# A GQA and gMLP block on one core: the second unit's queries a slot earlier, the second chunk's norm in two parts, and the last output tile in halves

## The chip, the cores and the metric

The kernel runs on one core of a Trainium2 chip. The metric is the device time of one launch in microseconds (us), the median of several runs. TensorE (PE) does the matmuls, ScalarE (ACT) the exponentials, VectorE (DVE) most copies out of PSUM and the norms, GpSimd (POOL) some small steps, and SyncE (SP) issues nearly all DMAs. Each engine works through its own instructions in program order.

## The reference, cut to what matters

```python
mod = (silu(c) @ w_mod)                        # sa, ca, ga, sb, cb, gb: 512 values each
h = layernorm(x) * (1 + ca) + sa               # x: 2048 x 512
x = x + ga * A(h)                              # attention: 32 query heads, 8 key/value heads of 128,
                                               # 2048 cached keys; wq 512 x 4096, wo 4096 x 512
h = layernorm(x) * (1 + cb) + sb
x = x + gb * B(h)                              # gMLP:
    z  = gelu(h @ w_in)                        #   512 x 1792
    z1, z2 = z[:, :896], layernorm(z[:, 896:])
    B  = (z1 * (w_sp @ z2 + b_sp)) @ w_out     #   w_sp 2048 x 2048, w_out 896 x 512
```

## The kernel before, in words

**Units and slots.** The 2048 rows are cut into 16 tiles of 128, four tiles make a chunk of 512 (`CT = 4`). Attention is 128 units: key/value group g (of 8) by tile j, with the group's four query heads together. The main loop runs over iterations `it` (0 to 133), each of eight slots. In a slot stand, in this order: what was put down for it with `at(it, slot, fn)` (kept in `later`), the score matmuls and the exponential of unit `it` (`qk`, s_ps banks, two of them), a part of the probabilities-times-values matmuls of an earlier unit (`pv`, `pv_rows`, o_ps banks), the `fill` of the slot (the query projections, `qproj`, misc banks), and the output projection of an earlier unit (`wo_proj`, misc banks). The schedule is manual: each engine runs its instructions in exactly this order, and an engine that waits holds back all that is behind it on its queue.

**Two kinds of units.** Units 5 to 121 go by rows in two cases of three: ACT writes the probabilities by rows, and SP turns them with four DMA transposes per unit (`turn_rows`, line 1088). The other units work by columns and need no such turn, but their outputs are turned (line 1147).

**The start.** Chunk 0 is normalised in pieces so that unit 0 can begin early. Queries of tiles 2 and 3 (`rest_q`) are projected as 16 matmuls of 256 columns in the fills of iteration 1, and DVE copies them to `qT` (line 978) in two parts. Chunks 1 to 3 go through `ln1_at`: statistics, `ln1_norm` (four normalised tiles `xn1`), a slot later `ln1_dma` (four DMA transposes from SP into `hT`, line 836), later `ln1_dma_mod` (DVE scales and shifts the whole chunk in place, four instructions, line 805 through `ln1_mod`). For chunk 1 these stand in (0, 7), (1, 2), (1, 3) and (2, 2). The query projection of chunk 1 starts in the fill of (2, 5) and ends in (3, 4). A load of 2 MB of modulation weights (`wmod_b`, which lies in the tile `wsp`; line 1312) stands at (1, 4) on the same SP queue.

**The second norm.** In the last group, `ln2` normalises each finished tile: `first` takes the statistics, `second` (slot 4 of the next iteration) normalises to `xn2` on DVE and turns it by DMA from SP to `xnT2` (line 1219), `third` (an iteration later, slot 3) modulates it on DVE (line 1226).

**The end.** The last 512 rows of the gMLP are worked off in a part of 384 columns and a part of 128 (`spatial`, 16 matmuls and one for the bias each). For the last 128, seven steps f make `yT[:, f]` on DVE (line 1573), and `o2_mm` sums seven matmuls of 512 columns into one bank; `finish_tile` multiplies by `gb_rows` (line 1590), adds x (line 1591) and issues the output's DMA from ACT's queue.

Of the kernel before, what the change touches and what calls it, by code (L numbers as in the profile page):

```python
# [10 lines left out]
BF16 = mybir.dt.bfloat16  # L11
FP32 = mybir.dt.float32
ACT = mybir.ActivationFunctionType
ALU = mybir.AluOpType
AX = mybir.AxisListType
P = 128
# [559 lines left out]
def kernel(  # L576
# [19 lines left out]
    nc = tc.nc  # L596
    _, S, D = A_x.shape
# [7 lines left out]
    NT = S // P  # L605
    NDT = D // P
    NKT = SK // P
    NFT = FH // P
    NCH = S // 512
    CT = 512 // P  # L610
# [8 lines left out]
    out_dram = out[0].rearrange("(t p) d -> p t d", p=P)  # L619
# [26 lines left out]
    x_sb = res.tile([P, NT, D], BF16, name="x_sb")  # L646
    ga_rows = res.tile([P, D], FP32, name="ga_rows")
    gb_rows = res.tile([P, D], FP32, name="gb_rows")
# [20 lines left out]
    def bank(name):  # L669
        return psum.tile([P, 512], FP32, name=name)  # L670
# [4 lines left out]
    def rstd_of(mv, n, tag):  # L675

        ve = stat.tile([P, CT], FP32, name=f"ve_{tag}")
        nc.gpsimd.tensor_scalar(
            out=ve[:, :n], in0=mv[:, :, 1], scalar1=LN_EPS, scalar2=None, op0=ALU.add
        )  # L680
        rstd = stat.tile([P, CT], FP32, name=f"rstd_{tag}")
        nc.gpsimd.tensor_tensor(out=rstd[:, :n], in0=ve[:, :n], in1=mhalf[:, :n], op=ALU.pow)
        return rstd

    def normalise(dst, src, mv, rstd):
        nc.vector.tensor_scalar(
            out=dst,
            in0=src,
            scalar1=mv,
            scalar2=rstd,  # L690
            op0=ALU.subtract,
            op1=ALU.mult,
        )

    def ln_stats(mv, j, src):
        st = stat.tile([P, 1, nc.vector.BN_STATS_DIM], FP32, name="bnst")
        nc.vector.bn_stats(out=st[:, 0, :], in_=src)
        nc.vector.bn_aggr(out=mv[:, j, :], in_=st[:])
# [87 lines left out]
    def ln1_stats(j0, n):  # L786
        for j in range(j0, j0 + n):
            ln_stats(mv1, j, x_sb[:, j, :])
        return rstd_of(mv1[:, j0 : j0 + n, :], n, "ln1")

    def ln1_norm(j0, n, rstd):
        xns = []
        for j in range(j0, j0 + n):
            xn = res.tile([P, D], BF16, name="xn1", bufs=4)
            normalise(xn[:], x_sb[:, j, :], mv1[:, j, 0:1], rstd[:, j - j0 : j - j0 + 1])
            xns.append(xn)
        return xns

    def hT_of(ch):
        if ch not in hTs:  # L800
            hTs[ch] = res.tile([P, NDT, 512], BF16, name="hT", bufs=NCH)
        return hTs[ch]

    def ln1_mod(dst, src, dt, engine=nc.vector):
        engine.tensor_scalar(
            out=dst,
            in0=src,
            scalar1=modc[:, NDT + dt : NDT + dt + 1],
            scalar2=modc[:, dt : dt + 1],
            op0=ALU.mult,  # L810
            op1=ALU.add,
        )
# [20 lines left out]
    def ln1_dma(j0, n, xns):  # L833
        hT = hT_of(j0 // CT)
        for jj in range(n):
            nc.sync.dma_start_transpose(out=hT[:, :, jj * P : (jj + 1) * P], in_=xns[jj][:])

    def ln1_dma_mod(ch):
        for dt in range(NDT):
            ln1_mod(hTs[ch][:, dt, :], hTs[ch][:, dt, :], dt)  # L840
# [79 lines left out]
    for dt in range(NDT):  # L920
        dst, src = hTs[0][:, dt, 0:P], xT0[:, dt * P : (dt + 1) * P]
        if dt == 1:
            nc.scalar.activation(
                out=dst,
                in_=src,
# [56 lines left out]
    first = {}  # L982
# [30 lines left out]
    def at(it, slot, fn):  # L1013
        later.setdefault((it, slot), []).append(fn)
# [191 lines left out]
    def ln2(it, j):  # L1206

        st = {}

        def first():  # L1210
            if j < NT - CT:
                ln_stats(mv2, j, x_sb[:, j, :])
            st["rstd"] = rstd_of(mv2[:, j : j + 1, :], 1, "ln2")

        def second():
            xn = res.tile([P, D], BF16, name="xn2", bufs=2)
            normalise(xn[:], x_sb[:, j, :], mv2[:, j, 0:1], st["rstd"][:, 0:1])
            st["xnT"] = res.tile([P, NDT, P], BF16, name="xnT2", bufs=2)
            nc.sync.dma_start_transpose(out=st["xnT"][:], in_=xn[:])

        def third():
            ch, c0 = j // CT, (j % CT) * P
            if ch not in h2Ts:
                h2Ts[ch] = res.tile([P, NDT, 512], BF16, name="hT", bufs=NCH)
            for dt in range(NDT):
                nc.vector.tensor_scalar(
                    out=h2Ts[ch][:, dt, c0 : c0 + P],
                    in0=st["xnT"][:, dt, :],
                    scalar1=modc[:, 4 * NDT + dt : 4 * NDT + dt + 1],
                    scalar2=modc[:, 3 * NDT + dt : 3 * NDT + dt + 1],  # L1230
                    op0=ALU.mult,
                    op1=ALU.add,
                )

        at(it + 1, 0 if j >= NT - CT else 2, first)
        at(it + 1, 4, second)
        at(it + 2, 3, third)

    mod_b = {}
# [40 lines left out]
    fill = {}  # L1280
# [16 lines left out]
    fill[0, 4], fill[0, 5] = next_q[0:8], next_q[8:16]  # L1297
    rest_q = qproj(0, [0, 1], 2 * P, 2 * P) + qproj(0, [2, 3], 2 * P, 2 * P)
    for i in range(6):
        fill[1, i + 1] = rest_q[(8 * i + 2) // 3 : (8 * i + 10) // 3]  # L1300

    def ln1_at(ch, stats, norm, turn):
        st = {}
        at(*stats, lambda: st.update(r=ln1_stats(ch * CT, CT)))
        at(*norm, lambda: st.update(x=ln1_norm(ch * CT, CT, st["r"])))
        at(norm[0], norm[1] + 1, lambda: ln1_dma(ch * CT, CT, st["x"]))
        at(*turn, lambda: ln1_dma_mod(ch))

    ln1_at(1, (0, 7), (1, 2), (2, 2))
    ln1_at(2, (2, 4), (3, 1), (4, 5))  # L1310
    ln1_at(3, (3, 5), (4, 1), (5, 5))
    at(1, 4, lambda: nc.sync.dma_start(out=wmod_b, in_=wmod_dram[:, :, 2 * D : NMOD]))
# [34 lines left out]
    for g in range(1, HKV):  # L1347
        it = (g - 1) * NT
# [6 lines left out]
        last = it - 1  # L1355
        for from_it, load in loads:
# [3 lines left out]
            last = next(u for u in pauses if u >= it + from_it and u > last)  # L1360
# [94 lines left out]
    for it in range(NU + 6):  # L1455
# [34 lines left out]
        for u in wos:  # L1490
            if u >= (HKV - 1) * NT:
                ln2(it, u % NT)
        if it == NU + 2:
            free_b.close()
            mlp = fast.enter_context(tc.tile_pool(name="mlp", bufs=1, side="right"))
            zs["z1T"] = mlp.tile([P, NFT, S], BF16, name="z1T")
            wout_sb = mlp.tile([P, NFT, D], BF16, name="wout_sb")
# [14 lines left out]
    for f in range(NFT):  # L1512
# [6 lines left out]
        out=ok1[:], in0=rall[:], scalar1=1.0 / SAFE, scalar2=None, op0=ALU.is_ge  # L1519
# [8 lines left out]
        out=bad[:], in0=okm[:], scalar1=-1.0, scalar2=1.0, op0=ALU.mult, op1=ALU.add  # L1528
# [48 lines left out]
    def o2_mm(dst, yT, jj, f):  # L1577
        nc.tensor.matmul(  # L1578
            dst,
            lhsT=yT[:, f, jj * P : (jj + 1) * P],  # L1580
            rhs=wout_sb[:, f, :],
            start=(f == 0),
            stop=(f == NFT - 1),
        )

    def finish_tile(t, jj, src):
        j = t * CT + jj
        tmp = mlp.tile([P, D], FP32, name="tmp", bufs=2)[:].bitcast(BF16)[:, 0:D]
        yout = mlp.tile([P, D], BF16, name="yout", bufs=2)
        nc.vector.tensor_tensor(out=tmp[:], in0=src, in1=gb_rows[:], op=ALU.mult)  # L1590
        nc.vector.tensor_tensor(out=yout[:], in0=tmp[:], in1=x_sb[:, j, :], op=ALU.add)
        nc.scalar.dma_start(out=out_dram[:, j, :], in_=yout[:])
# [3 lines left out]
    def o2_tile(t, jj):  # L1596
        o2 = bank("o_ps")
        for f in range(NFT):
            o2_mm(o2[:], yTs[t], jj, f)
        finish_tile(t, jj, o2[:])  # L1600

    last = NCH - 1
# [16 lines left out]
    o2_last = [acc[jj // 2][:, (jj % 2) * 512 : (jj % 2 + 1) * 512] for jj in range(CT)]  # L1619
    yT = yTs[last]  # L1620
    for f in range(NFT):
        spatial(last, yT, f, 0, n_a)
        if f < CT:
            o2_tile(last - 1, f)
        if f > 0:
            for jj in range(CT - 1):
                o2_mm(o2_last[jj], yT, jj, f - 1)
    redo = nc.values_load(flag[0:1, 0:1], min_val=0, max_val=P)
    for f in range(NFT):
        spatial(last, yT, f, n_a, P, bias_by_pe=True)  # L1630
        if f == 0:
            for jj in range(CT - 1):
                o2_mm(o2_last[jj], yT, jj, NFT - 1)
        elif f < CT:
            o2_mm(o2_last[CT - 1], yT, CT - 1, f - 1)
        if f % 2 == 0 and f < 2 * (CT - 1):
            finish_tile(last, f // 2, o2_last[f // 2])
    for f in range(CT - 1, NFT):
        o2_mm(o2_last[CT - 1], yT, CT - 1, f)
    finish_tile(last, CT - 1, o2_last[CT - 1])  # L1640
    fast.close()

    with tc.If(redo != 0):
# [34 lines left out]
```

## Time and profile before

| | |
|---|---|
| median of 3 runs | 1306.26 us (1305.87 to 1306.64) |
| the profiled execution's own time | 1306.41 us |
| its span in the trace | 1304.6 us |
| PE busy | 1287.9 us, 99% |
| ACT busy | 1113.4 us, 85% |
| DVE busy | 684.1 us, 52% |
| DMA queue of SP (q1) | 87.0% of 16 engines' span |

The profile is one execution. An engine is busy while an instruction runs on it; overlapping matmuls count once. A row of the timeline gives start, length, engine, line, operation, output and inputs, shapes and count, and in brackets the idle time before it with what ended it. `SPq` rows are the issue of a DMA by SP, not its transfer; the time from issue to landing is listed with the DMA issues. A row that merges several instructions has their count at its end.

### The profile page before, as it was taken

Reading aid. Unit: us, or ns where it says so; the run is one execution under the profiler, and the core shown is the slowest. Engines: PE = TensorE matmul, PEld = TensorE weight load, DVE = VectorE, ACT = ScalarE, POOL = GpSimd, SP = SyncE. Lnnn points to the kernel's source line nnn. Section 1 sums busy time; section 2 is a strip of 40 time slices with the busy share of each in tenths; the row PEclk is TensorE's granted clock in tenths of the full one; section 3 lists DMA queues with packets and bytes.
Section 4 is the critical chain, followed back from the end, with each engine's and each line's share of the span. In section 5 each row is a group of like instructions: output and inputs, shape, how many; then the busy total and the mean of one; then the engine's idle time right before and its main releaser. Section 6 shows DMA issues by size and latency. Waiting matters only on the chain.

```text
span 1304.6 us, 22478 instructions
## 1 busy us (share of the span) xinstructions
PE 1287.9 (99%) x8472; PEld 698.1 (54%) x8626; DVE 684.1 (52%) x1772; ACT 1113.4 (85%) x1683; POOL 57.4 (4%) x93
## 2 busy tenths in 40 slices
PE   8999999999999999999999999999999999999998
PEld 6655555555555555555555555555555556644445
DVE  5635445544554455445544554455445566784443
ACT  7999999999999999999999999999999998650000
POOL 1000000000000000000000000000000133410000
PEclk9999999999999999999999999999999999999999
DMA  7899899999999999999999999999999983264300
GB/s 187 183 198 189 157 190 182 190 170 189 181 194 168 188 173 184 183 181 183 185 188 173 183 187 189 172 185 176 177 198 163 168 151 90 49 137 98 81 21 31
DMA packets 774982, 211.19 MB, mean 162 GB/s; under 512 B 759248, under 2 KB 773200, under 8 KB 774864
## 3 DMA queue, kind: packets, MB, share of 16 engines
q1 hardware_dynamic: 772416, 207.55, 87.0%
q10 hardware_dynamic: 2448, 2.10, 0.5%
q8 instruction: 70, 1.15, 0.4%
q14 instruction: 48, 0.39, 0.1%
HBM read 21.37 MB, written 2.10 MB: 18 GB/s over the span
## 4 chain that ended last, share of the span: by engine, by line
PE 95%; DVE 2%; ACT 1%; DMA 1%; issue 1%; POOL 0%; SPq 0%; ACTq 0%
PE s_ps L1031 21%; PE o_ps L1103 20%; PE o_ps L1124 14%; PE s_ps L1068 13%; PE misc L1181 8%; PE misc L967 8%; PE misc L1545 7%; PE o_ps L1578 1%; PE s_ps L1411 1%; PE s_ps L1372 1%; DVE stz L1394 1%; PE s_ps L1578 0%; DMA wmod_a<-in_w_mod_dram 0%; ACT pT L1075 0%; DMA xnT<-xn 0%
## 5 line engine op out<-in xcount | busy, mean ns | idle before, releaser
L1031 PE MATMUL s_ps<-kT,qT 128*128 128x512 bf16 x1219 | 364.9, 379 | 2.3
L1038 ACT ACTIVATE win_sb<-s_ps 128x1024 bf16<-128x1024 f32 x312 | 319.2, 1024 | 3.8 <-PE s_ps L1031 0.7
L1103 PE MATMUL o_ps<-pT,v 128*128 128x512 bf16 x909 | 272.5, 379 | 1.3
L1174 DVE SCALAR_TENSOR_TENSOR xacc<-misc,rall,xacc 128x512 f32<-128x512 f32 x304 | 227.4, 748 | 68.2 <-PE misc L1181 60.7
L1068 PE MATMUL s_ps<-qT,kT 128*128 128x512 bf16 x784 | 233.2, 379 | 1.9 <-ACT pT L1075 1.1
L1075 ACT ACTIVATE pT<-s_ps 128x1024 bf16<-128x1024 f32 x216 | 217.8, 1025 | 12.9 <-PE s_ps L1068 4.9
L1038 ACT ACTIVATE pn<-s_ps 128x1024 bf16<-128x1024 f32 x208 | 213.0, 1024 | 2.0 <-PE s_ps L1031 0.5
L1103 PEld LDWEIGHTS <-v 128*128 128x128 bf16 x1248 | 122.1, 98 | 147.3
L1075 ACT ACTIVATE wsp<-s_ps 128x1024 bf16<-128x1024 f32 x176 | 179.9, 1024 | 12.1 <-PE s_ps L1068 4.2
L1181 PE MATMUL misc<-wo_g,oT 128*128 128x512 bf16 x479 | 181.5, 379 | 1.0
L967 PE MATMUL misc<-hT,wq_g 128*128 128x512 bf16 (+2 forms) x499 | 179.6, 370 | 0.5
L1031 PEld LDWEIGHTS <-qT 128*128 128x128 bf16 x1248 | 121.5, 98 | 109.4 <-issue 0.4
L978 DVE CAST qT<-misc 128x512 bf16<-128x512 f32 x127 | 87.2, 687 | 151.2 <-PE misc L967 151.2
L1124 PEld LDWEIGHTS <-pT 128*128 128x128 bf16 x1792 | 119.6, 98 | 50.5
L1092 DVE TENSOR_TENSOR tot<-rs 128x1 f32<-128x1 f32 x312 | 48.4, 155 | 171.5 <-ACT win_sb L1038 115.2
L1124 PE MATMUL o_ps<-v,pT 128*128 128x129 bf16 x1792 | 137.5, 220 | 0.6
L1068 PEld LDWEIGHTS <-kT 128*128 128x128 bf16 x784 | 75.6, 98 | 83.0 <-DVE qT L978 1.5
L1124 PEld LDWEIGHTS <-wsp 128*128 128x128 bf16 x1408 | 94.3, 98 | 41.5
L1124 PE MATMUL o_ps<-v,wsp 128*128 128x129 bf16 x1408 | 108.5, 220 | 0.5
L1038 ACT ACTIVATE wmod_a<-s_ps 128x1024 bf16<-128x1024 f32 x104 | 106.4, 1024 | 0.4 <-PE s_ps L1031 0.4
L1545 PE MATMUL misc<-wsp,z 128*128 128x512 bf16 (+2 forms) x554 | 100.1, 336 | 0.4
L1103 PE MATMUL o_ps<-wsp,v 128*128 128x512 bf16 x292 | 87.8, 379 | 0.4
(111 smaller groups left out, 874.3 us busy)
## 6 DMA issues: line engine op xcount, KB each, us to landing
wo_g<-in_A_wo_dram SPq DMA_DIRECT2D x8, 512.0 KB, 5.0
wq_g<-in_A_wq_dram SPq DMA_DIRECT2D x7, 512.0 KB, 4.0
v<-in_A_v_cache_dram SPq DMA_DIRECT2D x7, 512.0 KB, 4.5
wsp<-in_w_mod_dram SPq DMA_DIRECT2D x1, 2048.0 KB, 8.7
out_dram<-yout ACTq DMA_DIRECT2D x16, 128.0 KB, 1.7
pT<-win_sb SPq DMA_TRANSPOSE x117, 4.8
win_sb<-in_B_w_in_dram SPq DMA_DIRECT2D x1, 1792.0 KB, 8.0
x_sb<-in_A_x_dram SPq DMA_DIRECT2D x3, 512.0 KB, 7.0
```

What stands on the lines that cost most here:

```text
L967: nc.tensor.matmul(ps[0][:, o0 : o0 + n], lhsT=wqs[g][:, dt, hh * DH : (hh + 1) * DH], rhs=hTs[ch][:, dt, c0 : c0 + n], start=(dt == 0), s ...
L978: nc.vector.tensor_copy(out=dst, in_=src)
L1031: nc.tensor.matmul(s_ps[:, c * 512 : (c + 1) * 512], lhsT=qTs[b][:, hh, jj * P : (jj + 1) * P], rhs=groups[g]["kT"][:, k0 : k0 + 512], sta ...
L1038: nc.scalar.activation(out=rows_of(u, hh)[:, half * HK : (half + 1) * HK], in_=s_ps[:], func=ACT.Exp, scale=inv_sqrt_dh, accum_out=rsums[u ...
L1068: nc.tensor.matmul(s_ps[:, h * 512 : (h + 1) * 512].rearrange("p (r q) -> p r q", r=REP), lhsT=groups[g]["kT"][:, kt * P : (kt + 1) * P], ...
L1075: nc.scalar.activation(out=pTs[u][:, 2 * i : 2 * i + 2, :], in_=s_ps[:].rearrange("p (k q) -> p k q", k=2), func=ACT.Exp, scale=inv_sqrt_dh,)
L1092: nc.vector.tensor_tensor(out=tot[:], in0=rs[:, 2 * hh : 2 * hh + 1], in1=rs[:, 2 * hh + 1 : 2 * hh + 2], op=ALU.add)
L1103: nc.tensor.matmul(o_pss[u][:], lhsT=groups[g]["v1"][:, kt, 0:DH], rhs=pTs[u][:, kt, :], start=(kt == 0), stop=(kt == NKT - 1),)
L1124: nc.tensor.matmul(o_ps[:, hh % 2, 0 : DH + 1], lhsT=pTs[u][:, kt, hh * P : (hh + 1) * P], rhs=groups[g]["v1"][:, kt, 0 : DH + 1], start=( ...
L1174: nc.vector.scalar_tensor_tensor(out=xa[:], in0=X_ps[:], scalar=scale, in1=xa[:], op0=ALU.mult, op1=ALU.add)
L1181: nc.tensor.matmul(ps[0][:], lhsT=oTs[u][:, hh, :], rhs=groups[g]["wo"][:, hh, :], start=(hh == 0 or each), stop=(hh == REP - 1 or each),)
L1545: nc.tensor.matmul(g_pss[f][:, :n], lhsT=z2[:, st, f * P : (f + 1) * P], rhs=wsp[t][:, st, c0 : c0 + n], start=(st == 0), stop=(st == NT - ...
```

## The change

- The fills of `rest_q` move from slots 1 to 6 of iteration 1 to slots 0 to 5.
- Chunk 1's norm no longer goes through `ln1_at`. Two tiles are normalised and their two DMA transposes issued at (1, 3), the other two at (1, 6). `ln1_dma` now takes a column offset. Statistics and `ln1_dma_mod` stay at (0, 7) and (2, 2). The 2 MB load stays at (1, 4), so two of the four transposes now stand behind it on SP's queue.
- `ln2`: the DMA transpose moves from `second` (slot 4) to a step of its own, `turn`, in slot 5.
- The last tile's seven matmuls of 512 columns become 14 of 256, in two banks (the second an o_ps bank); the last ones run in the order given. DVE multiplies by halves, then adds and stores the whole tile.

```diff
     def ln1_dma(j0, n, xns):
         hT = hT_of(j0 // CT)
         for jj in range(n):
-            nc.sync.dma_start_transpose(out=hT[:, :, jj * P : (jj + 1) * P], in_=xns[jj][:])
+            c0 = (j0 + jj) % CT * P
+            nc.sync.dma_start_transpose(out=hT[:, :, c0 : c0 + P], in_=xns[jj][:])
...
         def second():
             xn = res.tile([P, D], BF16, name="xn2", bufs=2)
             normalise(xn[:], x_sb[:, j, :], mv2[:, j, 0:1], st["rstd"][:, 0:1])
+            st["xn"] = xn
+
+        def turn():
             st["xnT"] = res.tile([P, NDT, P], BF16, name="xnT2", bufs=2)
-            nc.sync.dma_start_transpose(out=st["xnT"][:], in_=xn[:])
+            nc.sync.dma_start_transpose(out=st["xnT"][:], in_=st["xn"][:])
...
         at(it + 1, 4, second)
+        at(it + 1, 5, turn)
         at(it + 2, 3, third)
...
     for i in range(6):
-        fill[1, i + 1] = rest_q[(8 * i + 2) // 3 : (8 * i + 10) // 3]
+        fill[1, i] = rest_q[(8 * i + 2) // 3 : (8 * i + 10) // 3]
...
-    ln1_at(1, (0, 7), (1, 2), (2, 2))
+    at(0, 7, lambda: first.update(r=ln1_stats(CT, CT)))
+    at(1, 3, lambda: first.update(x=ln1_norm(CT, 2, first["r"])))
+    at(1, 3, lambda: ln1_dma(CT, 2, first["x"]))
+    at(1, 6, lambda: first.update(y=ln1_norm(CT + 2, 2, first["r"][:, 2:CT])))
+    at(1, 6, lambda: ln1_dma(CT + 2, 2, first["y"]))
+    at(2, 2, lambda: ln1_dma_mod(1))
...
+    halves = [slice(hf * D // 2, (hf + 1) * D // 2) for hf in range(2)]
+    o2_half_ps = [o2_last[CT - 1][:, 0 : D // 2], bank("o_ps")[:, 0 : D // 2]]
+
+    def o2_half(hf, f):
+        nc.tensor.matmul(
+            o2_half_ps[hf],
+            lhsT=yT[:, f, (CT - 1) * P : CT * P],
+            rhs=wout_sb[:, f, halves[hf]],
+            start=(f == 0),
+            stop=(f == NFT - 1),
+        )
...
         elif f < CT:
-            o2_mm(o2_last[CT - 1], yT, CT - 1, f - 1)
+            for hf in range(2):
+                o2_half(hf, f - 1)
...
-    for f in range(CT - 1, NFT):
-        o2_mm(o2_last[CT - 1], yT, CT - 1, f)
-    finish_tile(last, CT - 1, o2_last[CT - 1])
+    for hf, f in ((0, 3), (0, 4), (0, 5), (1, 3), (1, 4), (0, 6), (1, 5), (1, 6)):
+        o2_half(hf, f)
+    j_end = NT - 1
+    tmp = mlp.tile([P, D], FP32, name="tmp", bufs=2)[:].bitcast(BF16)[:, 0:D]
+    yout = mlp.tile([P, 512], BF16, name="gb", bufs=2)
+    for hf in range(2):
+        nc.vector.tensor_tensor(
+            out=tmp[:, halves[hf]], in0=o2_half_ps[hf], in1=gb_rows[:, halves[hf]], op=ALU.mult
+        )
+    nc.vector.tensor_tensor(out=yout[:], in0=tmp[:], in1=x_sb[:, j_end, :], op=ALU.add)
+    nc.scalar.dma_start(out=out_dram[:, j_end, :], in_=yout[:])
```

## The prediction

> **What bounds the kernel now.** I read the page first, then the waits, then the timeline around each edit, then the landing times of the DMAs there.
>
> ```profile
> span 1304.6 us, 22478 instructions
> PE 1287.9 (99%) x8472; PEld 698.1 (54%) x8626; DVE 684.1 (52%) x1772; ACT 1113.4 (85%) x1683; POOL 57.4 (4%) x93
> PEld L1068 <- DVE qT L978: 1.5, 1, 1.5
> DVE hT L805 <- DMA hT<-xn: 4.6, 1, 4.6
> ```
>
> TensorE is busy 1287.9 of 1304.6 us. So work taken off another engine is worth nothing, and any wait on TensorE's own queue lengthens the span in full. The last two rows are waits between 14 and 60 us: PE's weight load stands 1.5 us for a query copy just as unit 2 begins, the only moment in that stage at which PE's queues wait; and DVE stands 4.6 us for the transposes of chunk 1, which PE does not feel. The first is what the start edit can take away; the second is what it puts at risk.
>
> **The start.** The timeline of that stage:
>
> ```profile
> 23.36 1.38 DVE L686 TENSOR_SCALAR xn<-x_sb,mv,rstd_ln 128x512 bf16<-128x512 bf16 x4 [0.98 <-POOL rstd_ln L682]
> 23.80 5.90 SPq L836 DMA_TRANSPOSE hT<-xn  x4
> 25.79 0.68 DVE L978 CAST qT<-misc 128x512 bf16<-128x512 f32 x1
> 26.53 0.61 PE L1068 MATMUL s_ps<-qT,kT 128*128 128x512 bf16 x2 [1.05 <-ACT pT L1075]
> 27.23 5.60 ACT L1075 ACTIVATE pT<-s_ps 128x1024 bf16<-128x1024 f32 x6 [0.70 <-PE s_ps L1068]
> 29.75 0.59 SPq L1312 DMA_DIRECT2D wsp<-in_w_mod_dram  x1
> 30.43 8.06 SPq L1147 DMA_TRANSPOSE oT<-onorm  x2
> 31.04 1.38 DVE L805 TENSOR_SCALAR hT<-hT,modc 128x512 bf16<-128x512 bf16 x4 [4.57 <-DMA hT<-xn]
> 31.94 0.59 PE L967 MATMUL misc<-hT,wq_g 128*128 128x512 bf16 x2
> ```
>
> DVE norms four tiles before it copies queries; the second copy ends at 25.79 + 0.68 = 26.47 and PE starts unit 2 at 26.53. With the fills a slot earlier, the copy stands behind two norms instead of four and its matmuls end about a slot sooner, so unit 2 starts when ACT frees a bank: ACT's idle 0.70 us is the most that can go. I put the gain at 0.5, since the fill that now stands in slot 0 delays unit 1's second scores a little. It is worth this only if nothing stops PE later, and something does.
>
> Chunk 1's query projection starts at 31.94, behind DVE's modulation, which starts at 31.04 when the last of four transposes has landed; its first quarter takes 1.38 / 4 = 0.35. PE's slack there is thus about 0.5 us. After the change SP's order is two transposes, the 2 MB load, the other two transposes, then oT. What a transpose behind that load costs, the trace of before shows once, with the oT at 30.43:
>
> ```profile
> 23.80 3.27 SPq L836 DMA_TRANSPOSE hT<-xn  x2
> wsp<-in_w_mod_dram SPq DMA_DIRECT2D x1, 2048.0 KB, 8.7
> oT<-onorm SPq DMA_TRANSPOSE x1, 9.8
> DMA to landing us min/median/max: 2.4/2.4/4.6
> DMA packets 490, 0.13 MB, mean 125 GB/s; under 512 B 490, under 2 KB 490, under 8 KB 490
> DMA packets 100, 0.41 MB, mean 410 GB/s; under 512 B 0, under 2 KB 0, under 8 KB 100
> DMA packets 154, 0.39 MB, mean 395 GB/s; under 512 B 61, under 2 KB 61, under 8 KB 154
> ```
>
> The first row is SP's issue of two of the transposes; the next two are issue to landing of the load and of that oT; the fourth is the same for the twelve transposes of hT. The last three are what moved in 28 to 29, 35 to 36 and 36 to 37 us. A transpose is 0.13 MB in small packets, some 1 us of transfer, and lands 2.4 us after its issue. Behind the load it took 9.8: up to 36 us only large packets moved, and the oT's first small ones came when the load drained. The queue is worked off in order.
>
> So: two transposes issue by 23.80 + 3.27 = 27.07, the load at 27.1 instead of 29.75, and it lands at 27.1 + 8.7 = 35.8. The third transpose lands as the oT did, 30.43 + 9.8 - (29.75 + 8.7) = 1.8 after the load, at 37.6; the fourth one transfer later, about 0.8, at 38.4. DVE waits for it at (2, 2), and with DVE wait everything behind on its queue: unit 1's normalisation, chunk 2's statistics, the query copies. PE runs on to the fill of (2, 5) and stands there until 38.4 + 0.35 + 0.1 = 38.85, against 31.94: **+6.9 us**. The 0.5 gained ahead of it only makes PE wait longer. Nothing later gives this back: PE has no other wait up to 60 us in which to catch up, and ACT, which runs behind PE's scores, goes idle meanwhile. Bounds: the small packets came from 36 to 37 us on, up to 2 us before the load had landed; if both transposes slip into that tail, the fourth lands about 36.9 and PE loses 5.4; if the two queue behind each other with the oT's whole 1.8 each, 39.4 and 7.9. I take the value between, from the oT's own row.
>
> Then PE has stood for some 7 us, and how it restarts no row of the middle shows. The nearest is the kernel's beginning:
>
> ```profile
> 1.18 4.87 PE L777 MATMUL o_ps<-onorm 128*128 128x512 bf16 x11 [1.18 <-DVE onorm L768]
> 3.00:4.00 1.00, 1.00 (x4) 0.31 (x3) 0.89 (x4) 0.21 (x1) 0.00 (x0) 1.00 0.89 293
> 1283.47 0.81 PE L1578 MATMUL s_ps<-wout_sb,yT 128*128 128x512 bf16 x3
> ```
>
> Eleven matmuls of 512 columns took 4.87 us after idleness, 0.44 each; late in the kernel three take 0.81, of which the last one alone 0.38, so 0.215 each. The granted clock in the windows stands at 1.00 (the last but two number) even then, so the spacing shows this and not that column. PE lost 4.87 - 11 x 0.215 = 2.5 us in that start. The stage after (2, 5) is full of PE work, so the same slow stretch would cost **+2.5**; the other end is 0, if 7 us of standing does not slow it. I take 2.5, the only row there is. [...]
>
> **The second norm's turn.** On SP's queue, the slot between lets one transpose of probabilities pass ahead of xnT in three iterations; everywhere else the order is as it was. One such place is tight:
>
> ```profile
> 1061.01 1.86 SPq L1219 DMA_TRANSPOSE xnT<-xn  x1
> 1062.96 3.04 SPq L1088 DMA_TRANSPOSE pT<-wmod_a  x1
> 1065.90 0.98 DVE L1226 TENSOR_SCALAR hT<-xnT,modc 128x128 bf16<-128x128 bf16 x4 [1.44 <-DMA xnT<-xn]
> 1066.80 0.68 DVE L978 CAST qT<-misc 128x512 bf16<-128x512 f32 x1
> 1067.53 0.38 PE L1181 MATMUL misc<-wo_g,oT 128*128 128x512 bf16 x1
> 1066.00:1068.00 2.00, 2.00 (x11) 0.82 (x9) 2.00 (x7) 1.95 (x3) 0.00 (x0) 1.00 1.13 206
> ```
>
> DVE already waits 1.44 us for xnT, then copies queries until 1066.80 + 0.68 = 1067.48, and PE's matmul into a misc bank starts at 1067.53, right behind: no slack. A transpose of 0.5 MB at 206 GB/s (the last number) is 2.5 us of transfer ahead of xnT. PE then loses between 0 (the queue has a gap there that absorbs it) and 2.5; I take the middle, **+1.2**. The first of the three, and below it the second:
>
> ```profile
> 1034.10 1.60 SPq L1219 DMA_TRANSPOSE xnT<-xn  x1
> xnT<-xn SPq DMA_TRANSPOSE x1, 2.8
> 1038.25 0.97 DVE L1226 TENSOR_SCALAR hT<-xnT,modc 128x128 bf16<-128x128 bf16 x4
> 1039.14 0.68 DVE L978 CAST qT<-misc 128x512 bf16<-128x512 f32 x1
> 1041.27 0.38 PE L1181 MATMUL misc<-wo_g,oT 128*128 128x512 bf16 x1
> 1048.74 1.19 SPq L1219 DMA_TRANSPOSE xnT<-xn  x1
> 1055.69 0.97 DVE L1226 TENSOR_SCALAR hT<-xnT,modc 128x128 bf16<-128x128 bf16 x4
> ```
>
> The first landed at 1036.9, 1.3 ahead of its use; 2.5 later makes DVE 1.1 late, and the copy that frees a misc bank ends at 1040.9, still ahead of PE's next request for one at 1041.27. The second is issued 7 us ahead of its use. Both cost nothing; without that cover the first would add up to 1.1, which the upper end's full 2.5 at the tight place allows for.
>
> **The last tile.**
>
> ```profile
> 1298.75 0.29 DVE L1573 TENSOR_TENSOR yT<-misc,z1T 128x128 bf16<-128x128 f32 x1 [0.35 <-PE misc L1565]
> 1299.62 0.69 DVE L1590 TENSOR_TENSOR tmp<-s_ps,gb_rows 128x512 bf16<-128x512 f32 x1 [0.57 <-PE s_ps L1578]
> 1300.34 0.42 DVE L1591 TENSOR_TENSOR yout<-tmp,x_sb 128x512 bf16<-128x512 bf16 x1
> 25.45 0.42 DVE L1136 TENSOR_TENSOR onorm<-o_ps,rall 128x256 bf16<-128x256 f32 x1
> ```
>
> The last yT is ready at 1299.04, so the first half's last matmul can start about 1299.1 and end near 1299.4 instead of 1299.6. Two half multiplications of 0.42 follow one another, then the same addition of 0.42: the end comes at about 1300.65 instead of 1300.76, **-0.1**. The seven added matmuls split columns that were there; their weight loads run beside other matmuls. If three of them show, it is +0.2.
>
> **Sum.** 6.9 + 2.5 + 1.2 - 0.1 = 10.5, on the profiled execution's own time of 1306.41, which lies 0.15 above the median of the runs; on the median, 1306.26 + 10.5 = **1316.8 us**. A measurement here tells from no change about 0.2%, 2.6 us.
>
> **Rivals.**
>
> *PE restarts at full speed.* All else as above: 1306.26 + 6.9 + 1.2 - 0.1 = 1314.3, down to 1306.26 + 5.4 - 0.1 = 1311.6 with the lower bounds and no loss at xnT. For it: the granted clock stays at 1.00 in every window. Against: it did so in the slow start too. Chance 0.24.
>
> *The transposes are not held by the load* (not slower). If their small packets are served beside the load's large ones, each lands 2.4 after its issue. Four issues took 5.90 and two 3.27, so 1.3 each; behind the load's issue of 0.59 the fourth is issued at about 29.0 and lands at 31.4. PE then starts chunk 1's queries at 31.85, 0.1 earlier than before, xnT falls in its gap, and the time is 1306.26 - 0.1 - 0.1 = 1306.1, no measurable change. Each us that it lands later is a us lost; from a landing at 34 on it would measure as slower. Against: the 9.8 and the packet sizes. Chance 0.08.
>
> *DVE's backlog bites again.* DVE resumes with four modulations, the statistics of chunk 2 and two copies to do; if a misc bank is freed later than PE asks for it, PE stands a second time by 1 to 3 us, and 1316.8 becomes about 1319. In before, DVE and PE kept the same distance after 31.94, which speaks against. Chance 0.07.
>
> **How the numbers follow.** The forecast has 0.61. The range goes from 1311.6 to 1306.26 + 7.9 + 2.5 + 2.5 = 1319.2, which leaves out the rival without a hold and part of the backlog. Faster by over 0.2%: 0.02, since even the whole 0.70 and the last tile are under 2.6 us; within 0.2%: 0.08; slower: 0.90.
>
> **What would show it.** In the profile after: the load issued near 27.1; hT's slowest landing near 9 us instead of 4.6; a DVE wait of about 12 us at line 805's chunk modulation, up from 4.6; PE idle for about 7 us before the projection of chunk 1, with the 512-column matmuls behind it at 0.44 instead of 0.215 for some us; at about 1075 us a PE wait of 0 to 2.5 on a misc bank. If hT's landings stay under 4 us and PE has no idle stretch by 40 us, the prediction is wrong at its main term.

## The result, and the profile after

The changed kernel takes 1314.18 us (median of 6 runs, 1313.04 to 1314.94) against 1306.45 us before (6 runs, 1305.87 to 1306.96): a ratio of 1.0059, 95% interval 1.0046 to 1.0072. It is 7.7 us slower. Its profiled execution took 1314.26 us with a span of 1312.4, which is 7.8 more than before.

The page of the changed kernel, and from its waits the three that before did not have at this length (PE's own for the whole span, DVE's between 15 and 60 us; the columns are us in total, times, longest):

```profile
span 1312.4 us, 22494 instructions
PE 1290.6 (98%) x8481; PEld 700.1 (53%) x8633; DVE 685.1 (52%) x1773; ACT 1113.4 (85%) x1683; POOL 57.5 (4%) x93
PE misc L968 <- DVE hT L805: 5.1, 1, 5.1
PE misc L1182 <- DVE qT L979: 1.0, 1, 1.0
DVE hT L805 <- DMA hT<-xn: 10.2, 1, 10.2
```

PE has 2.7 us more busy time, though it multiplies no more columns, and two new waits of 5.1 and 1.0 us. The timeline of the start (lines have moved by one: 967 is now 968):

```profile
24.10 0.69 DVE L979 CAST qT<-misc 128x512 bf16<-128x512 f32 x1
25.87 0.59 PE L1069 MATMUL s_ps<-qT,kT 128*128 128x512 bf16 x2 [0.32 <-ACT pT L1076]
26.39 0.58 SPq L1322 DMA_DIRECT2D wsp<-in_w_mod_dram  x1
27.07 2.65 SPq L837 DMA_TRANSPOSE hT<-xn  x2
30.88 0.61 PE L1125 MATMUL o_ps<-v,pT 128*128 128x129 bf16 x8
36.13 1.38 DVE L805 TENSOR_SCALAR hT<-hT,modc 128x512 bf16<-128x512 bf16 x4 [10.16 <-DMA hT<-xn]
36.60 1.01 PE L968 MATMUL misc<-hT,wq_g 128*128 128x512 bf16 x2 [5.10 <-DVE hT L805]
37.40 1.06 PE L1069 MATMUL s_ps<-qT,kT 128*128 128x512 bf16 x2
39.12 1.06 PE L968 MATMUL misc<-hT,wq_g 128*128 128x512 bf16 x2
41.90 0.59 PE L1069 MATMUL s_ps<-qT,kT 128*128 128x512 bf16 x2
```

Unit 2 starts at 25.87 instead of 26.53, so the step that was meant to be quicker is. Then PE stands from 31.49 (30.88 + 0.61) to 36.60, because DVE's modulation starts at 36.13 instead of 31.04. A pair of matmuls then takes 1.01 to 1.06 us and no longer 0.59, until about 41.2. Chunk 1's query projection starts 4.7 us later than before (36.60 against 31.94); its sixth matmul is followed by scores at 41.90 against 35.01, 6.9 later. The row of before:

```profile
35.01 0.59 PE L1068 MATMUL s_ps<-qT,kT 128*128 128x512 bf16 x2
```

The step from 4.7 to 6.9, 2.2 us, is the slow stretch.

The windows of that stretch (us, then busy time and count of PE, PEld, DVE, ACT and POOL, the granted clock, the DMA share and GB/s):

```profile
33.00:34.00 1.00, 0.00 (x0) 0.00 (x0) 0.00 (x0) 0.00 (x0) 0.00 (x0) 1.00 0.99 330
34.00:35.00 1.00, 0.00 (x0) 0.00 (x0) 0.00 (x0) 0.00 (x0) 0.00 (x0) 0.69 1.47 174
40.00:41.00 1.00, 1.00 (x5) 0.44 (x4) 0.97 (x3) 0.00 (x0) 0.00 (x0) 0.50 0.00 0
41.00:42.00 1.00, 0.95 (x11) 0.77 (x10) 0.93 (x5) 0.93 (x1) 0.58 (x2) 0.89 0.00 0
```

The clock is halved: a mean of 0.69 in 34 to 35 puts the fall at about 34.4, and 0.89 in 41 to 42 puts the return at about 41.2.

The landings (load, all four transposes, and the fourth alone):

```profile
wsp<-in_w_mod_dram SPq DMA_DIRECT2D x1, 2048.0 KB, 8.6
DMA to landing us min/median/max: 2.4/5.0/8.5
hT<-xn SPq DMA_TRANSPOSE x1, 7.6
```

The load lands at 26.39 + 8.6 = 35.0, the third transpose at 27.07 + 8.5 = 35.6, the fourth, issued at 28.4, at 36.0.

The second norm's turn, at the place that had no slack:

```profile
1066.77 2.66 SPq L1089 DMA_TRANSPOSE pT<-wmod_a  x1
1069.52 1.57 SPq L1223 DMA_TRANSPOSE xnT<-xn  x1
1073.79 0.98 DVE L1230 TENSOR_SCALAR hT<-xnT,modc 128x128 bf16<-128x128 bf16 x4 [2.43 <-DMA xnT<-xn]
1074.68 0.68 DVE L979 CAST qT<-misc 128x512 bf16<-128x512 f32 x1
1075.42 0.38 PE L1182 MATMUL misc<-wo_g,oT 128*128 128x512 bf16 x1 [0.96 <-DVE qT L979]
```

The transpose of probabilities goes first, DVE waits 2.43 us instead of 1.44, and PE waits 0.96 for the bank that the query copy frees. Relative to before this matmul is 7.89 us late (1075.42 against 1067.53), up from 6.90 some us ahead of it (1067.82 against 1060.92).

The end:

```profile
1306.65 0.29 DVE L1583 TENSOR_TENSOR yT<-misc,z1T 128x128 bf16<-128x128 f32 x1 [0.35 <-PE misc L1575]
1307.32 0.42 DVE L1667 TENSOR_TENSOR tmp<-s_ps,gb_rows 128x256 bf16<-128x256 f32 x1 [0.38 <-PE s_ps L1642]
1307.66 0.42 DVE L1667 TENSOR_TENSOR tmp<-o_ps,gb_rows 128x256 bf16<-128x256 f32 x1
1308.11 0.42 DVE L1670 TENSOR_TENSOR gb<-tmp,x_sb 128x512 bf16<-128x512 bf16 x1
```

From the last yT to the end of the addition it takes 1.88 us (1306.65 to 1308.53) against 2.01 before (1298.75 to 1300.76): -0.13. So 4.7 + 2.2 + 1.0 - 0.1 = 7.8, the whole difference of the spans.

### The profile page after: what moved, and what is told of

Read it like the earlier page. It is cut to its first block, busy times and chain, and to the rows that moved or that the text cites. A ratio compares the mean times of both kernels' runs of the same rounds, so it can differ in the third digit from the quotient of the medians.

```text
span 1312.4 us, 22494 instructions
## 1 busy us (share of the span) xinstructions
PE 1290.6 (98%) x8481; PEld 700.1 (53%) x8633; DVE 685.1 (52%) x1773; ACT 1113.4 (85%) x1683; POOL 57.5 (4%) x93
## 4 chain that ended last, share of the span: by engine, by line
PE 96%; DVE 1%; DMA 1%; ACT 1%; issue 1%; POOL 0%; SPq 0%; ACTq 0%; DVEq 0%
PE s_ps L1032 20%; PE o_ps L1104 20%; PE o_ps L1125 14%; PE s_ps L1069 12%; PE misc L1182 8%; PE misc L968 8%; PE misc L1555 7%; PE s_ps L1382 2%; PE s_ps L1421 2%; PE o_ps L1588 1%; DMA hT<-xn 1%; PE o_ps L777 0%; PE s_ps L1588 0%; DMA xnT<-xn 0%; ACT pn L1039 0%
```

## The experiments

Nine kernels were run, each timed against the kernel before on the same chip.

**The load behind all four transposes.** In the changed kernel:

```diff
-    at(1, 4, lambda: nc.sync.dma_start(out=wmod_b, in_=wmod_dram[:, :, 2 * D : NMOD]))
+    at(1, 7, lambda: nc.sync.dma_start(out=wmod_b, in_=wmod_dram[:, :, 2 * D : NMOD]))
```

> The changed kernel with one line different: the 2 MB load stands at (1, 7), behind all four transposes of chunk 1. Queue theory (the transposes behind the load hold DVE, DVE holds PE, and the standstill then costs clock as well): the whole loss of the start goes, the gain of about 0.5 us there shows, and what is left is the wait of about 1.0 us at the second norm's turn and -0.1 at the end: about +0.4 us against before, 1306.8. Rival (the split of the norm and the earlier fills cost in themselves, by DVE's order): the 6.9 us stay, about 1314.

1306.65 us (10 runs, 1306.25 to 1306.78), ratio 1.0002 (0.9992 to 1.0011). The timeline:

```profile
29.95 0.60 SPq L1322 DMA_DIRECT2D wsp<-in_w_mod_dram  x1
30.95 0.59 PE L968 MATMUL misc<-hT,wq_g 128*128 128x512 bf16 x2
```

PE does not stand, and no matmul is slow. One line takes away 7.5 of the 7.7 us; the rest of the rebuilt start costs nothing. Its PE wait of 1.1 us at the turn is still there. No run put the load on another engine's queue, so whether it would hold the transposes from there too is not shown.

**Only the load between the transposes.** In the kernel before, with the column offset in `ln1_dma`:

```diff
-    ln1_at(1, (0, 7), (1, 2), (2, 2))
+    at(0, 7, lambda: first.update(r=ln1_stats(CT, CT)))
+    at(1, 2, lambda: first.update(x=ln1_norm(CT, CT, first["r"])))
+    at(1, 3, lambda: ln1_dma(CT, 2, first["x"][0:2]))
+    at(1, 5, lambda: ln1_dma(CT + 2, 2, first["x"][2:4]))
+    at(2, 2, lambda: ln1_dma_mod(1))
```

> The kernel before with one thing different: two of the four transposes of chunk 1 are issued at (1, 5), behind the load at (1, 4). The norm stays whole at (1, 2), the fills, the second norm and the end are as before. Queue theory: PE stands from about 31.9 to 36.6 us and restarts at half rate for some 4.6 us: +4.7 + 2.2 = +6.9, about 1313.2. Rival (the other parts of the start make the loss): no change, 1306.3.

1314.04 us (4 runs, 1313.49 to 1314.27), ratio 1.0058 (1.0041 to 1.0075).

```profile
36.94 1.01 PE L968 MATMUL misc<-hT,wq_g 128*128 128x512 bf16 x2 [5.20 <-DVE hT L805]
39.47 1.06 PE L968 MATMUL misc<-hT,wq_g 128*128 128x512 bf16 x2
42.04 0.68 PE L968 MATMUL misc<-hT,wq_g 128*128 128x512 bf16 x2
```

SP's order alone makes the loss, 0.8 more than expected: the wait ends 0.3 later than in the changed kernel (36.94, 5.0 behind before) and the slow stretch lasts to about 42.2. It costs 2.5 here: the scores behind the sixth matmul come at 42.55, 7.5 behind before.

**PE kept busy while it would stand.** In the changed kernel, 22 matmuls of 512 columns whose result nothing reads:

```diff
+    def busy(n):
+        b_ps = bank("misc")
+        for k in range(n):
+            nc.tensor.matmul(b_ps[:], lhsT=ones_bf[:], rhs=hTs[0][:, 0, :], start=True, stop=True)
...
+    fill.setdefault((2, 4), []).append(lambda: busy(22))
```

> The changed kernel with 22 matmuls of 512 columns added at the end of the fill of (2, 4), into a bank that nothing reads: 22 x 0.215 = 4.7 us of PE work inside the standstill. Clock theory (standing still makes PE slow afterwards): the matmuls behind the wait run at 0.215 instead of 0.43 us, the granted clock stays at 1.00 there, and 2.2 of the 7.8 us go: about 1312.0. Rival (the slow stretch comes from DVE or DMA work at that time, or from waiting as such): no gain, 1314.2 or later.

1311.82 us (4 runs, 1311.43 to 1312.33), ratio 1.0042 (1.0026 to 1.0059).

```profile
30.45 4.91 PE L988 MATMUL misc<-hT,ones_bf 128*128 128x512 bf16 x22
36.62 0.70 PE L968 MATMUL misc<-hT,wq_g 128*128 128x512 bf16 x2 [0.38 <-DVE hT L805]
38.04 0.59 PE L968 MATMUL misc<-hT,wq_g 128*128 128x512 bf16 x2
38.00:39.00 1.00, 1.00 (x10) 0.53 (x8) 0.97 (x4) 0.81 (x1) 0.00 (x0) 1.00 0.00 0
39.79 0.59 PE L1075 MATMUL s_ps<-qT,kT 128*128 128x512 bf16 x2
PE misc L1188 <- DVE qT L979: 0.5, 1, 0.5
```

The projection starts at 36.62 as in the changed kernel, but the next pair comes 1.4 us later and not 2.5, and the clock stays at 1.00. With 22 more matmuls the kernel is 2.4 us quicker. In the traces the spans differ by 2.6 (1309.8 against 1312.4): the scores behind the sixth matmul come 2.1 earlier (39.79 against 41.90), which is the slow stretch, and the other 0.5 is a shorter wait at the second norm's turn (0.5 instead of 1.0). The load lands at 35.0 and DVE's modulation starts at 36.15, as in the changed kernel, so the slow stretch follows from PE's standing and not from DVE's or the DMAs' work at that time.

**Three quarters, and half, of the load ahead.** In the changed kernel (3 or 2 for `k`):

```diff
-    at(1, 4, lambda: nc.sync.dma_start(out=wmod_b, in_=wmod_dram[:, :, 2 * D : NMOD]))
+    at(1, 4, lambda: nc.sync.dma_start(out=wmod_b[:, 0:k, :], in_=wmod_dram[:, 0:k, 2 * D : NMOD]))
+    at(1, 7, lambda: nc.sync.dma_start(out=wmod_b[:, k:NDT, :], in_=wmod_dram[:, k:NDT, 2 * D : NMOD]))
```

> The changed kernel with three quarters of the load (1.5 MB) at (1, 4) and the last quarter at (1, 7). Queue theory: a quarter is 0.52 MB at the 410 GB/s of the trace, 1.3 us, so the last transpose lands 1.3 us sooner and PE stands 1.3 us less; if the clock still falls in a standstill of some 3.7 us, +7.8 - 1.3 = +6.5, 1312.8; if it does not, +4.3, 1310.6. Rival (a transpose behind any load waits for a fixed time, or the size does not matter): 1314.2.

1312.45 us (4 runs: 1311.80 and 1311.89, 1313.01 and 1313.19), ratio 1.0048 (1.0032 to 1.0065).

```profile
34.87 0.70 PE L968 MATMUL misc<-hT,wq_g 128*128 128x512 bf16 x2 [3.78 <-DVE hT L805]
35.00:36.00 1.00, 1.00 (x4) 0.34 (x3) 0.96 (x5) 0.00 (x0) 0.00 (x0) 0.78 0.52 205
38.00:39.00 1.00, 1.00 (x7) 0.48 (x5) 0.96 (x3) 0.09 (x1) 0.00 (x0) 0.51 0.00 0
```

> The changed kernel with half of the load (1 MB) at (1, 4) and the other half at (1, 7). Queue theory: the last transpose lands 2 x 1.3 = 2.6 us sooner than in the changed kernel and PE stands about 2.1 us longer than before at that place. If a standstill of some 2.5 us leaves the clock alone: 2.1 + 1.0 - 0.1 = +3.0, 1309.4. If the clock falls after any standstill of this kind: +5.2, 1311.6. If the size of the load does not matter: 1314.2.

1310.10 us (6 runs, 1309.21 to 1311.34), ratio 1.0030 (1.0018 to 1.0042).

```profile
33.73 0.70 PE L968 MATMUL misc<-hT,wq_g 128*128 128x512 bf16 x2 [2.27 <-DVE hT L805]
35.15 0.59 PE L968 MATMUL misc<-hT,wq_g 128*128 128x512 bf16 x2
```

PE's wait goes 5.1, 3.8, 2.3 us for four, three and two quarters: 1.3 to 1.5 us for each 0.52 MB, as expected. The clock is the part with two answers. After 3.8 us of waiting it fell, though only at about 35.6 (0.78 in 35 to 36), when PE had already been at work for 0.7 us, and returned at 39.0: 3.4 us at half rate, against 6.8 in the changed kernel (34.4 to 41.2). The four runs lie in two groups, 1311.80 and 1311.89 at a mean granted clock of 0.998, 1313.01 and 1313.19 at 0.997; the trace is of the first group, and what the clock did in the second no trace shows. After 2.3 us it stayed in the profiled execution. The six runs of that kernel lie in two groups: 1309.21 to 1309.57 at a mean granted clock of 0.999, and 1310.62 to 1311.34 at 0.998, about 1.5 us apart; the profiled execution is of the first group. So the longer runs are those of the lower mean clock; that the clock fell in them behind this standstill is inferred from that, and no trace shows it.

**Only the second norm's turn.** In the kernel before, `turn` in slot 5 as in the change, and nothing else.

> The kernel before with only the second norm's turn a slot later. Queue theory (a transpose of 0.5 MB passes ahead of xnT in three places, one of them without slack): a PE wait of about 1.0 us on a misc bank near 1068 us, +1.0, 1307.4. Rival (the wait of the changed kernel there came from the shift by the start): no wait, 1306.4.

1307.47 us (11 runs, 1307.18 to 1307.72), ratio 1.0008 (0.9998 to 1.0017). The interval holds 1, but every run is above all 28 of before (1306.00 to 1306.91), and the trace shows the wait at its place:

```profile
1067.02 0.98 DVE L1229 TENSOR_SCALAR hT<-xnT,modc 128x128 bf16<-128x128 bf16 x4 [2.51 <-DMA xnT<-xn]
1068.65 0.38 PE L1181 MATMUL misc<-wo_g,oT 128*128 128x512 bf16 x1 [1.05 <-DVE qT L978]
```

**Only the end.** In the kernel before, the halves of the last tile, and nothing else.

> The kernel before with only the last tile in halves. Theory: -0.1 us from the last wait to the last addition's end, which the traces show and the times hardly can: 1306.3. Rival (the added weight loads or the second bank cost): up to +0.2, 1306.6.

1306.20 us (11 runs, 1305.98 to 1306.64), ratio 0.9999 (0.9990 to 1.0008). The difference of 0.2 is of the expected sign, and no larger than the times can resolve.

**What is left when both losses are undone.** The changed kernel with the load at (1, 7) and `turn` in slot 4.

> The changed kernel with the load at (1, 7) and the second norm's turn back in slot 4: the earlier fills, the split norm and the halves are all that is left of the change. Theory: -0.5 at the start and -0.1 at the end, 1305.8, under both kernels. Rival (the earlier PE start of unit 2 is given back at the next query projection): -0.1, 1306.3.

1305.70 us (11 runs, 1305.31 to 1305.79), ratio 0.9994 (0.9985 to 1.0003). The interval does not exclude 1; all its runs are below all 28 of before. PE starts unit 2 behind ACT alone, and the next projection at 31.06 against 31.94 before. Of these 0.9 us, 0.3 was there ahead of the step that changed (the norm of chunk 1 starts at 23.07 against 23.36):

```profile
25.60 0.59 PE L1069 MATMUL s_ps<-qT,kT 128*128 128x512 bf16 x2 [0.32 <-ACT pT L1076]
31.06 0.59 PE L968 MATMUL misc<-hT,wq_g 128*128 128x512 bf16 x2
```

**Only the earlier fills.** In the kernel before, `fill[1, i]` instead of `fill[1, i + 1]`.

> The kernel before with only the fills of iteration 1 a slot earlier; the norm of chunk 1 stays whole at (1, 2), the load behind its four transposes. Theory A (the earlier matmuls make the gain): both query copies stand behind the four norms that end near 24.7, so the second ends near 26.1 and PE waits 0.2 us for it instead of 0.6 behind the bank: -0.3 to -0.4, 1306.0. Theory B (the split norm makes the gain, since the copies wait for DVE and not for PE): no gain, 1306.4. The version with both, measured at 1305.7 with the halves at the end, is the comparison.

1305.89 us (11 runs, 1305.52 to 1306.37) against 1306.41 (14 runs, 1306.03 to 1306.83), ratio 0.9997 (0.9988 to 1.0006).

```profile
24.39 1.28 DVE L978 CAST qT<-misc 128x512 bf16<-128x512 f32 x2
25.73 0.60 PE L1068 MATMUL s_ps<-qT,kT 128*128 128x512 bf16 x2 [0.43 <-DVE qT L978]
```

This speaks for theory A: most of the gain comes without the split, -0.5 in the medians, though the interval holds 1 and the two groups of runs overlap. In the trace unit 2 starts 0.8 earlier than before, of which 0.3 was there ahead of the step (the norm starts at 23.09 against 23.36). Both copies run back to back behind the whole norm, and PE waits 0.43 us for the second. Since the norm and its transposes stay together, nothing comes to stand behind the load. What the split adds is within the spread of the runs.

## Why the prediction was right, and where its sizes were off

The measured 1314.18 lies in the range of 1311.6 to 1319.2, the direction and the mechanism are those forecast, and the point of 1316.8 is 2.6 us too high.

- **The hold by the load** (+6.9 predicted, +4.7 measured). The chain of steps was as written: transposes behind the load, DVE behind the transposes, PE behind DVE, nothing given back later. The term was mis-sized, and even its lower bound of 5.4 was too high. DVE's start was put at 38.4 and came at 36.1. Of the 2.3 us, 0.7 is the load's issue, 26.39 instead of 27.1: two transposes took SP 3.27 us in one execution and 2.6 in the other. The other 1.6 is the way from the load's landing to the fourth transpose's. The prediction took 1.8 for the first transpose behind the load, from the one oT in the trace, and 0.8 for the next; they took 0.6 and 0.4. Their small packets moved ahead of the load's landing at 35.0, as the packets of the changed kernel in 33 to 34 and in 34 to 35 us show:

```profile
DMA packets 267, 0.33 MB, mean 330 GB/s; under 512 B 198, under 2 KB 198, under 8 KB 267
DMA packets 623, 0.17 MB, mean 174 GB/s; under 512 B 617, under 2 KB 617, under 8 KB 623
```

So the case of the lower bound came, both transposes in the load's tail: there the fourth lands 1.1 behind the load (36.9 against 35.8), measured 1.0, and 5.4 less the 0.7 of the issue is the 4.7 measured. The oT's 1.8 was hardly a chance of one execution. With only the turn and with only the end, where the oT is again the one transpose behind the load for some 7 us, the two oT of that stage took 6.7 and 6.6 us to landing in the median, against 6.7 in before; in the changed kernel, as the third behind the load, it landed 0.4 after the fourth transpose of hT (29.81 + 6.6). Why a transpose alone there takes longer the runs do not settle.

- **The slow restart** (+2.5 predicted, +2.2 measured). The row of the kernel's beginning served as the price. The prediction was wrong in saying that the granted clock would not show it: it reads 0.50. Nor did the clock of before stay at 1.00 in every window, as was said for a restart at full speed: PE's last matmul there ends at 1299.58, and the clock reads 0.63 in 1303 to 1304 us and 0.50 from 1303.5 to the end. That the sizes agree is in part luck: the row at the beginning was taken at a granted clock of 1.00, while here PE was at work in 4.6 of the 6.8 us at half clock, and half of that is 2.3. The price was 2.5 with only the load between and 1.8 with three quarters of the load (behind its sixth matmul 4.7 late, at its first 2.9). The half-rate stretches last 6.8 us here (34.4 to 41.2), as long with only the load between (35.4, by 0.69 in 35 to 36, to about 42.2), and 3.4 with three quarters of the load (35.6 to 39.0). What sets their beginning and their length the runs do not show: the clock fell 2.9 us after PE began to stand in the changed kernel (34.4 against 31.49), 3.7 with only the load between (35.4 against 31.73), and 4.5 with three quarters of the load (35.6 against 31.08), there with PE at work again for 0.7 us.
- **The rival of a restart at full speed** stood at 1314.3, nearly the measured time, and is refuted: the clock fell. Its time was right because its hold was 2.2 us too long.
- **The turn** (+1.2 predicted, +1.0 measured, alone +1.1; in the other traces with this step PE waits 0.5 to 1.1). The middle of 0 and 2.5 was a guess that held; the other two places where the order changed cost nothing, as worked out.
- **The end** (-0.1 predicted, -0.13 measured), and **the start's own gain** (0.5 predicted as hidden behind the hold; about 0.5 to 0.6 when nothing holds, by traces and medians, and less than the times alone can resolve).
- **The transposes not held** and **DVE's backlog**: the first is refuted by the landings of 8.5 and 7.6 us; of the second there is no sign, as PE has no wait behind 36.60 in that stage.

## What to carry to other kernels

When a step is moved, list every DMA that it issues and look up what stands ahead of each on its queue: here two 0.13 MB transposes behind a 2 MB load cost 7 us, and moving the load by three slots gave it back. Price a PE standstill of some us with its slow restart (2.2 us here, behind a wait of 5.1), and see in the traces whether the clock fell. Of a bundle of small edits, run each alone: here the earlier fills alone seem to hold most of the gain, about 0.5 us and near what the times can resolve, and two other steps lost 8.

## What the runs showed of the hardware that was not expected

A standstill of PE can be made cheaper by giving it work that nobody needs: 22 such matmuls brought 2.1 us at that place. The clock can also fall after PE has resumed (at 35.6, with PE back at 34.87), so the end of a wait is not the end of its price. At the kernel's start matmuls of 512 columns take 0.44 us each, twice the 0.215 of later, while the granted clock reads 1.00; the runs do not tell why.
